# The layout of the first block's key and query loads, and the place of the iota, in a windowed attention kernel followed by a squared-ReLU MLP

## The chip, the cores and the metric

The kernel runs on one core of a Trainium2 chip. The metric is the device time of one execution in microseconds. The core has five engines that work through their own queues in order: PE (matmuls, with PEld for its weight loads), ACT (activations), DVE (vector work), POOL and SP. DMA transfers are issued from the queues of SP, ACT and POOL and are carried out by 16 DMA engines.

## The reference

Two layers in sequence. The first is causal attention with a window of 128 positions and a linear distance bias; the second is an MLP with a squared ReLU.

```python
batch, n_heads, seq, head_dim = (8, 8, 576, 64)
scores = scale * np.matmul(q, k.transpose(0, 1, 3, 2))
bias = slopes[:, None, None] * (-np.abs(rel))[None, :, :]
mask = (rel >= 0) & (rel < 128)
attn = softmax(np.where(mask, scores + bias, -1e9))
attn_out = np.matmul(attn, v)                        # 8 x 8 x 576 x 64
x = attn_out.transpose(0, 2, 1, 3).reshape(4608, 512)
out = np.maximum(x @ w_in, 0.0) ** 2 @ w_out         # 512 -> 2048 -> 512
```

All inputs and the output are float32 in DRAM; the kernel computes in bfloat16 with float32 accumulation.

## The kernel before, in words

**Blocks.** Each of the 8 batches has 576 positions, cut into blocks of 128 (the last one has 64). The kernel treats the first block of all batches first (blocks 0 to 7), then the others. For each block it loads k, q and v for all 8 heads. Blocks from 1 on are loaded by POOL's queue, which casts to bfloat16 on the way (L387 for k and q into `kq`, L392 for v into `vf` or `vt`). Block 0 is different: its k and q are loaded as float32 into `stage` by four transfers from the queues of SP and ACT (L373, one half r each), and DVE casts them into `kq` (L379). Its v comes from POOL like the others.

**From a block to x.** PE transposes `kq` (L443, group tp), ACT or DVE copies the result out of PSUM into `kqT` or `kqf` (L273, L271), PE computes the scores s (L499), ACT takes the exponential (L523), DVE multiplies with the masks (L531), PE multiplies with v (L566, group pv), DVE divides by the row sums (L584, L588), and PE transposes the result (L608, xp), which ACT or DVE copies into `xT`. From block 9 on, SP's transposing DMAs take the place of the PE transposes.

**The layout of block 0.** Its `kq` rows are not tokens. Each partition holds, for one head pair c and one group g of four neighbouring tokens, the 4 x 64 numbers of a head of the pair in each half r. So a row of `stage` is 1 KB of contiguous DRAM. `source` (L350) makes this view of DRAM, and the evacuation of the transposes (L451 to L458) puts the tokens back in order.

**The MLP.** Groups of 512 tokens go through w_in (L700 for the first three groups in narrower units, L716 afterwards), ACT's relu (L671), DVE's square (L662), w_out (L742), a copy to `osb` and a store by SP (L761). The weights are loaded in four quarters each by POOL, between the loads of the blocks, in the order of the list FIRST: b0, b1, b2, i0, i1, o0, i2, o1, b3, i3, o2, o3, b4 and so on, where b is a block, i a quarter of w_in and o one of w_out. Of b0, only v is on POOL's queue.

**What sets the order.** Every step is a task with a cost, a key and the tasks it depends on. A planner (L84) simulates the engines with these costs: at each turn it takes, among the tasks that could start within a small tolerance of the earliest, the one with the lowest key; where two engines could take a task at the same time and key, the first engine in its list gets it. The instructions are then emitted in the order of the planned starts, and each engine runs its own in that order. A DMA task is planned to follow the DMA tasks planned before it, one at a time (870 ns for a load of 128 rows from POOL, 330 ns for one of block 0's four loads). At most 8 DMAs are outstanding on POOL's side, and 8 on the side of SP and ACT. Where the planner sees a gap of more than 200 ns ahead of one of PE's early tasks, it puts filler matmuls on a zero tile there (L250 to L252), enough to fill 70% of the gap at full clock. Eight warm-up matmuls (L413) stand at the very start of PE's queue.

**The constants of the start.** `build_iota` (L286) writes the token distances on POOL. The identity for PE's transposes, the distance tile and through it the masks (L294, L300, L301, L310) are made from it by DVE and ACT. Its key is EARLY + IOTA (L290); v of block 0 has the key EARLY + 100.2, and the loads of block 1 EARLY + 200 and above.

Of the kernel before, what the change touches and what calls it, by code (L numbers as in the profile page):

```python
# [20 lines left out]
N_WARM = 8  # L21
FILL = 0.7
LEAD = 320
IOTA = 100.3
TP, XP = "h", "h"
UNITS = {0: 128, 1: 256, 2: 256}
CUT = 384
# [148 lines left out]
def kernel(  # L176
# [14 lines left out]
    C = d_model // 128  # L191
# [54 lines left out]
    def bank_of(slot, name):  # L246
        bank(slot, name)
        return slot

    def fill(task, slot):  # L250
        for _ in range(int(task.gap * FILL / 56.0) if task.gap > 200.0 else 0):
            nc.tensor.matmul(slot.tile[:, 0:128], warm[:, 0:128], warm[:, 0:128], start=True, stop=True)  # L252

    def tile_of(slot):
        return tiles[slot.tag][slot.idx]

    def act(n):
        return n * 0.95 + 115.0
# [4 lines left out]
    def dve_p(n, rate=1):  # L263
        return n / rate / 0.96 + 185.0

    def mm(n):
        return max(n, 66) / 2.4 + 2.5

    def copy(task, o, i):
        if task.eng == "DVE":  # L270
            nc.vector.tensor_copy(o, i)  # L271
        else:
            nc.scalar.activation(o, i, AF.Copy)  # L273
# [15 lines left out]

    t_iota = plan.add({"POOL": 400.0}, EARLY + IOTA, build_iota, name="iota")  # L290
    t_wz = plan.add({"DVE": 280.0}, EARLY, lambda: nc.vector.memset(warm, 0.0), name="warm0")
# [58 lines left out]
    def source(t, m, split=False):  # L350
        b, kb = seq[m]
        s = t[b, :, kb * 128:kb * 128 + blk[kb], :]
        if split:
            return s.rearrange("(c r) (g i) d -> c g r (i d)", r=2, i=4)
        return s.rearrange("h s d -> s h d")

    def load_block(m, key):
# [10 lines left out]
        if m == 0:  # L368
            t_l = []
            for i, src in enumerate((k, q)):  # L370
                for r, (eng, e) in enumerate((("SP", nc.sync), ("ACTQ", nc.scalar))):
                    def fetch(i=i, src=src, r=r, e=e):
                        e.dma_start(view(stage, i)[:, r], source(src, m, split)[:, :, r])  # L373
                    t_l.append(plan.add({eng: 450.0}, key + 0.1 * i, fetch, dma=330.0, lat=1000.0,
                                        name=f"l{'kq'[i]}{m}.{r}"))

            def cast_kq(i):
                w = slice(i * d_model, (i + 1) * d_model)
                nc.vector.tensor_copy(kq[s_kq[m].idx][:, w].rearrange("s (i r d) -> s r i d", i=4, d=D),  # L379
                                      stage[:, w].rearrange("s (r i d) -> s r i d", r=2, d=D))  # L380
            c_k = plan.add({"DVE": 480.0}, key, lambda: cast_kq(0), t_l[0:2], [s_kq[m]], name=f"ck{m}")
            c_q = plan.add({"DVE": 480.0}, key, lambda: cast_kq(1), t_l[2:4] + [c_k], name=f"cq{m}")
            t_kq[m] = [c_k, c_q]
        else:
            def fetch_kq():
                for i, src in enumerate((k, q)):
                    nc.gpsimd.dma_start(view(kq[s_kq[m].idx], i), source(src, m, split))  # L387
            t_kq[m] = [plan.add({"POOL": 1780.0}, key, fetch_kq, [], [s_kq[m]], dma=2 * ns,
                                name=f"lkq{m}", count=2)]

        def fetch_v():
            nc.gpsimd.dma_start(tile_of(s_v[m])[0:n, :, 0:D], source(v, m))  # L392
# [29 lines left out]
    def transpose_kq(m, due):  # L422
        n = blk[seq[m][1]]
        kb = seq[m][1]
        sT = s_kqT[m] = Slot("kqT" if kb else "kqT0")
        split = m == 0
        if m >= N_PE:
            def flip():
                nc.sync.dma_start_transpose(out=tile_of(sT)[:, :, 0:n], in_=kq[s_kq[m].idx][0:n, :])
            t_f = plan.add({"SP": 1500.0}, due - 60, flip, t_kq[m] + [t_zero if kb == HALF else None], [sT],  # L430
                           [s_kq[m]], dma=1700.0 * n / 128, name=f"kqT{m}")
            t_kqT[m] = [[t_f], [t_f]]
            return
        t_tp, evs = [None, None], [[], []]
        for i in range(2):
            st = Slot(TP if m else "o")

            def tp(i=i, st=st):
                fill(t_tp[i], bank_of(st, "tp"))
                st.tile = st.tile.bitcast(BF16)  # L440
                src = kq[s_kq[m].idx][:, i * d_model:(i + 1) * d_model]
                for j in range(C):
                    nc.tensor.transpose(st.tile[:, j * 128:(j + 1) * 128],  # L443
                                        src[:, j * 128:(j + 1) * 128], ident)
            t_tp[i] = plan.add({"PE": 4 * mm(128)}, due - 60 + i, tp,
                               [t_ident, t_tp[0] if i else last["tp"], t_kq[m][min(i, len(t_kq[m]) - 1)]],
                               [st] if i else [st, sT], [s_kq[m]] if i else [], name=f"tp{m}.{i}")

            pieces = [(0, C // 2), (C // 2, C)] if i and m == 0 else [(0, C)]
            for c0, c1 in pieces:  # L450
                def evac(i=i, st=st, c0=c0, c1=c1, e=len(evs[i])):  # L451
                    o = tile_of(sT)[:, i * C + c0:i * C + c1, 0:n]
                    if split:
                        src = st.tile[:, 0:512].rearrange("p (i c g) -> p c g i", i=4, c=C)[:, c0:c1]
                        o = o.rearrange("p c (g i) -> p c g i", i=4)
                    else:
                        src = st.tile[:, 0:512].rearrange("p (c s) -> p c s", c=C)[:, c0:c1, 0:n]
                    copy(evs[i][e], o, src)  # L458
                w = (c1 - c0) * n
                evs[i].append(plan.add({"ACT": act(w), "DVE": dve_p(w, 1 if split else 2)}, due - 58, evac,  # L460
                                       [t_tp[i]] + evs[i], [], [st], name=f"ev{m}.{i}"))
        last["tp"] = t_tp[1]
        t_kqT[m] = [[evs[0][0], evs[1][0]], evs[0] + evs[1]]
# [339 lines left out]
```

The softmax here doesn't subtract the row's maximum and nothing guards it: scores larger than these inputs give would overflow.

## Time and profile before

| what | value |
|---|---|
| three runs | 320.89, 321.00, 321.04 us (median 321.0) |
| the profiled execution | 320.97 us, span of its records 319.2 us |
| instructions | 7118 |
| DMA traffic | 39.14 MB in 164082 packets, mean 123 GB/s |
| k of block 0: issued by SP and ACT at | 0.74 us |
| q of block 0: issued by SP at, by ACT at | 1.53, 1.91 us |
| DVE's casts of k and q start at | 6.57, 10.63 us |
| first transposes of k and q on PE | 7.42, 11.11 us |
| first scores on PE | 12.61 us |
| first MLP matmuls (L700) | 19.07 us |
| POOL's start: v0, iota, k1, q1 | 1.25, 2.36, 2.66, 3.61 us |

The span counts from the first record of the profile to the last; the time of an execution is somewhat longer. The profile names groups by line, engine, operation and tiles. A name such as `PE h L700` stands for matmuls of line 700 that write the tile h. DMA share is the mean share of the 16 engines that is busy with packets; since several packets of one engine can be under way at once, it can go above 1. The chain of work is followed back from the last instruction: at each step to what released it or, without a wait, to the instruction before it on its engine.

### The profile page before, as it was taken

The page shows a single profiled execution, that of the slowest core. Times are in us where ns is not written, and L with a number is a line of the kernel's source. Part 1 is how long each engine was busy: PE and PEld are TensorE (multiplying, and loading weights), DVE is VectorE, ACT ScalarE, POOL GpSimd, SP SyncE. Part 2 cuts the span into 40 slices and gives each one's busy share as a digit, 9 for nine tenths or more (in the row PEclk, how much of TensorE's full clock was granted, in tenths as well). Part 3 has the DMA queues.
Part 4 walks back from the last instruction along what each step waited for, and adds up shares of the span by engine and source line. Part 5 has one row for each costly group of instructions (what it writes and reads, how often), then busy time and mean ns, then how long its engine had stood idle before and what let it go on. Part 6 is the DMA issues. An engine that isn't in the chain of part 4 may idle for free.

```text
span 319.2 us, 7118 instructions
## 1 busy us (share of the span) xinstructions
PE 304.4 (95%) x2778; PEld 177.4 (56%) x2820; DVE 172.7 (54%) x494; ACT 173.9 (54%) x340; POOL 105.4 (33%) x131
## 2 busy tenths in 40 slices
PE   5798999999999999999999999999999999999994
PEld 2597776767777755554555555554454444444442
DVE  2374566756766766767666666675664222222211
ACT  3376467658775547665665665655753444344300
POOL 8734498645440957203947006400000000000000
PEclk9999999999999999999999999999999999999999
DMA  8999999999999999949999929952121100010112
GB/s 96 174 204 190 179 156 184 152 169 141 206 165 145 159 171 205 163 69 148 169 195 167 135 69 157 184 132 61 42 65 36 49 34 33 35 33 34 66 68 66
DMA packets 164082, 39.14 MB, mean 123 GB/s; under 512 B 154704, under 2 KB 159568, under 8 KB 164048
## 3 DMA queue, kind: packets, MB, share of 16 engines
q0 software_dynamic: 114656, 18.10, 83.1%
q1 hardware_dynamic: 49128, 20.33, 32.5%
q8 instruction: 22, 0.36, 0.5%
q10 hardware_dynamic: 264, 0.26, 0.3%
q14 instruction: 12, 0.10, 0.1%
HBM read 36.70 MB, written 9.44 MB: 145 GB/s over the span
## 4 chain that ended last, share of the span: by engine, by line
PE 93%; DMA 3%; issue 1%; ACT 1%; DVE 1%; ACTq 0%
PE o L742 38%; PE h L716 26%; PE h L700 14%; PE pv L566 6%; PE s L499 6%; DMA stage<-in_q_dram 3%; PE tp L443 2%; PE xp L608 1%; PE pv L252 1%; ACT masks L310 0%; PE s L252 0%; ACTq L373 0%; ACT rt L671 0%; PE h L252 0%; DVE kq L379 0%
## 5 line engine op out<-in xcount | busy, mean ns | idle before, releaser
L742 PE MATMUL o<-w_out_sb,g 128*128 128x512 bf16 (+2 forms) x567 | 138.5, 373 | 2.4 <-issue 1.6
L671 ACT ACTIVATE rt<-h 128x512 bf16<-128x512 f32 x144 | 86.0, 610 | 93.0 <-PE h L716 65.4
L662 DVE TENSOR_TENSOR g<-rt 128x512 bf16<-128x512 bf16 x144 | 60.2, 421 | 75.7 <-ACT rt L671 75.6
L716 PE MATMUL h<-xT,w_in_sb 128*128 128x512 bf16 x367 | 95.5, 379 | 0.8
L742 PEld LDWEIGHTS <-g 128*128 128x128 bf16 x592 | 54.0, 98 | 55.6
L523 ACT ACTIVATE P<-s 128x512 bf16<-128x512 f32 (+1 forms) x136 | 67.1, 584 | 13.6 <-PE s L499 13.6
L716 PEld LDWEIGHTS <-w_in_sb 128*128 128x128 bf16 x384 | 35.2, 98 | 39.3
L531 DVE TENSOR_TENSOR P<-P,masks 128x512 bf16<-128x512 bf16 (+1 forms) x112 | 44.4, 405 | 14.3 <-ACT P L523 9.6
L700 PE MATMUL h<-xT,w_in_sb 128*128 128x128 bf16 (+1 forms) x512 | 46.7, 246 | 0.7 <-ACT rt L671 0.7
L392 POOL DMA_DIRECT2D vt<-in_v_dram x32 | 27.2, 851 | 57.6 <-PE pv L566 52.3
L387 POOL DMA_DIRECT2D kq<-in_k_dram x39 | 33.6, 861 | 24.7 <-DMA kqT<-kq 18.9
L700 PEld LDWEIGHTS <-w_in_sb 128*128 128x128 bf16 x512 | 38.7, 98 | 4.6 <-issue 0.8
L387 POOL DMA_DIRECT2D kq<-in_q_dram x39 | 33.7, 864 | 6.2 <-PE h L700 2.7
L588 DVE TENSOR_TENSOR x<-pv,rec 128x256 bf16<-128x256 f32 (+1 forms) x80 | 33.6, 422 | 2.6
L566 PEld LDWEIGHTS <-P 128*128 128x128 bf16 (+1 forms) x576 | 25.9, 101 | 14.8 <-DVE P L538 1.7
L584 DVE RECIPROCAL rec<-pv 128x4 f32<-128x4 f32 (+1 forms) x80 | 14.3, 179 | 20.8 <-PE pv L566 18.0
L566 PE MATMUL pv<-vt,P 128*128 128x65 bf16 (+1 forms) x448 | 24.6, 194 | 0.1
L273 ACT ACTIVATE osb<-o 128x512 f32<-128x512 f32 x23 | 14.0, 607 | 8.0 <-PE o L742 7.7
L499 PEld LDWEIGHTS <-kqT 64*128 64x128 bf16 x448 | 12.4, 94 | 7.3 <-issue 6.8
L271 DVE COPY osb<-o 128x512 f32<-128x512 f32 (+2 forms) x14 | 9.2, 654 | 12.8 <-PE o L742 12.6
L499 PE MATMUL s<-kqT 64*128 64x128 bf16 (+1 forms) x256 | 15.6, 210 | 0.0
L443 PE MATMUL tp<-ident,kq 128*128 128x128 bf16 x72 | 7.5, 239 | 4.8 <-DVE kq L379 4.8
(42 smaller groups left out, 110.2 us busy)
## 6 DMA issues: line engine op xcount, KB each, us to landing
out_dram<-osb SPq DMA_DIRECT2D x32, 256.0 KB, 3.6
kq<-in_k_dram POOLq DMA_DIRECT2D x31, 128.0 KB, 7.4
kq<-in_q_dram POOLq DMA_DIRECT2D x31, 128.0 KB, 7.4
vt<-in_v_dram POOLq DMA_DIRECT2D x24, 128.0 KB, 7.0
w_in_sb<-in_moe_w_in_dram POOLq DMA_DIRECT2D x4, 512.0 KB, 11.6
w_out_sb<-in_moe_w_out_dram POOLq DMA_DIRECT2D x4, 512.0 KB, 15.5
vf<-in_v_dram POOLq DMA_DIRECT2D x8, 128.0 KB, 9.0
out_dram<-osb SPq DMA_DIRECT2D x6, 128.0 KB, 2.3
```

Of the source, the lines that this page charges most:

```text
L387: nc.gpsimd.dma_start(view(kq[s_kq[m].idx], i), source(src, m, split))
L392: nc.gpsimd.dma_start(tile_of(s_v[m])[0:n, :, 0:D], source(v, m))
L499: nc.tensor.matmul(sS[2 * g2 + r].tile[:, jj * 256 + c0:jj * 256 + c0 + w], tile_of(s_kqT[mk])[rows, c, :], tile_of(s_kqT[mq])[rows, C + c ...
L523: nc.scalar.activation(flat(Pt[sP.idx]), sS[i].tile.rearrange("p (j t) -> p j t", j=2)[:, :, lo:hi], AF.Exp, bias=0.0, scale=scale)
L531: nc.vector.tensor_tensor(flat(Pt[sP.idx]), flat(Pt[sP.idx]), flat(masks), op=ALU.mult)
L566: nc.tensor.matmul(sv.tile[0:n, hi * (D + 1):(hi + 1) * (D + 1)], Pt[sP.idx][:, place(h)].rearrange("p t q -> p (t q)")[:, w], tile_of(s_v ...
L588: nc.vector.tensor_tensor(xt[sx.idx][0:n, hf * 256:(hf + 1) * 256].rearrange("p (h e) -> p h e", h=4), heads(sv)[0:n, :, 0:D], sr.tile[0:n ...
L662: nc.vector.tensor_tensor(o, i, i, op=ALU.mult)
L671: nc.scalar.activation(srt.tile, slot.tile, AF.Relu, bias=0.0, scale=1.0)
L700: nc.tensor.matmul(slot.tile[:, f * w:(f + 1) * w], w_in_sb[:, cc, fc * 128:(fc + 1) * 128], xT[:, cc, lo:lo + w], start=cc == 0, stop=cc ...
L716: nc.tensor.matmul(slot.tile, w_in_sb[:, cc, fc * 128:(fc + 1) * 128], xT[:, cc, g * 512:(g + 1) * 512], start=cc == 0, stop=cc == C - 1)
L742: nc.tensor.matmul(slot.tile[:, 0:hi - lo], gt[:, fc, t * 128:(t + 1) * 128], w_out_sb[:, fc, lo:hi], start=fc == 0, stop=fc == FCB - 1)
```

## The change

Two things are changed. In the view of DRAM that block 0's k and q are loaded through, the partition dimension is made of the token group g (32 of them) outermost and the head pair c (4) inside it, where before c was outermost. Row p of `stage` was c * 32 + g and is g * 4 + c. The evacuation of the transposes reads PSUM's columns in the new order, so that `kqf` holds the same as before. The four transfers, their issuing queues, their row size of 1 KB and the casts stay.

Second, the key of the iota is EARLY + 3 instead of EARLY + 100.3. It stood behind the load of block 0's v on POOL's queue and ahead of block 1's loads; now it stands ahead of both.

```diff
-IOTA = 100.3
+IOTA = 3
...
         if split:
-            return s.rearrange("(c r) (g i) d -> c g r (i d)", r=2, i=4)
+            return s.rearrange("(c r) (g i) d -> g c r (i d)", r=2, i=4)
...
                     if split:
-                        src = st.tile[:, 0:512].rearrange("p (i c g) -> p c g i", i=4, c=C)[:, c0:c1]
+                        src = st.tile[:, 0:512].rearrange("p (i g c) -> p c g i", i=4, c=C)[:, c0:c1]
                         o = o.rearrange("p c (g i) -> p c g i", i=4)
```

## The prediction

> **What bounds the kernel now.** I read the page from the engine shares down to the chain that ended last, then that chain in order of time over the first 30 us.
>
> ```profile
> PE 304.4 (95%) x2778; PEld 177.4 (56%) x2820; DVE 172.7 (54%) x494; ACT 173.9 (54%) x340; POOL 105.4 (33%) x131
> ...
> PE 93%; DMA 3%; issue 1%; ACT 1%; DVE 1%; ACTq 0%
> ```
>
> PE sets the end. The one other engine with a share is DMA, 3%, and the lines give it to one transfer, the first block's queries. Busy time by stretch (columns: PE, PEld, DVE, ACT, POOL, clock, DMA share, GB/s) shows where PE is loose:
>
> ```profile
> 0.00:26.98 26.98, 20.16 (x227) 14.84 (x229) 12.27 (x57) 14.02 (x42) 16.26 (x24) 1.00 1.34 160
> 26.98:319.20 292.22, 284.27 (x2551) 162.60 (x2591) 160.47 (x438) 159.88 (x299) 89.15 (x108) 1.00 1.15 119
> ```
>
> From 26.98 us on PE is 97% busy, so nothing but PE work can be saved there. Before that it stands 6.8 us, and of its 20.2 busy us 6.5 are filler matmuls (the group of L252, 64 of them) and 3.6 the warm-up: some 17 us are no work. Only a shift of this prologue can come out at the end. Its chain (start, length, what):
>
> ```profile
> 1.91 8.69 DMA stage<-in_q_dram
> 10.61 0.02 issue
> 10.63 0.44 DVE kq L379
> 11.07 0.05 issue
> 11.11 0.61 PE tp L443 x4
> 11.72 0.96 PE s L252 x9
> 12.68 0.33 PE s L499 x4
> ...
> 26.45 0.49 ACT rt L671
> 26.94 0.04 issue
> 26.98 3.02 PE h L700 x51
> ```
>
> The q load holds everything until 10.6. The second limit is hidden in POOL's waits. At most 8 of its DMAs are outstanding, so the wait of the ninth shows when the first has landed:
>
> ```profile
> 11.06 0.74 POOL L340 DMA_DIRECT2D w_in_sb<-in_moe_w_in_dram  x1 [2.32 <-DMA vf<-in_v_dram]
> ...
> 18.29 0.76 POOL L340 DMA_DIRECT2D w_in_sb<-in_moe_w_in_dram  x1 [1.61 <-DMA w_in_sb<-in_moe_w_in_dram]
> ...
> 20.83 0.74 POOL L343 DMA_DIRECT2D w_out_sb<-in_moe_w_out_dram  x1 [1.79 <-DMA w_in_sb<-in_moe_w_in_dram]
> ...
> 26.18 0.88 POOL L387 DMA_DIRECT2D kq<-in_k_dram  x1 [2.05 <-DMA w_in_sb<-in_moe_w_in_dram]
> ```
>
> Counting in issue order (v0, k1, q1, v1, k2, q2, v2, in0, in1, out0, in2, ...): v0 landed near 11.0, in0 near 18.25, in1 near 20.8, in2 near 26.15. The first L700 matmuls, which read in0, start at 19.07; the next 16, on in1, at 21.20; those on in2 at 26.98. So the prologue has two ropes: the q load, and the weight stream only 0.4 to 0.8 us behind it.
>
> **What the Trainium skill says.** "DMA: Bandwidth & Descriptors", section "Why a DMA increments its semaphore by 16 and not by 1": a DMA runs on the largest k up to 16 engines that divides the slowest dimension of both sides. The old view has 4 outermost, the destination 128 partitions: k=4. The trace agrees: between 2.5 and 3.5 us, with only ACT's k half running, the mean DMA share is 0.18, under 3 of 16 engines. The same page, "Issuing engines are not separate DMA queues": all queues interleave on the same engines, so the four also carry POOL's loads. The trace agrees: with q landed at 10.6, packets under 512 B (only block loads have those) still run at 317 in 12 to 13 us and 238 in 14 to 15, and end near 15.4, while weight rows begin near 11: a few engines lag by about 4 us. "SBUF — State Buffer", section "Who interferes with whom": a DVE cast in a two-port mode and GpSimd block each other. Agreeing: the k cast beside POOL's issues took 0.80 us, the q cast with POOL waiting 0.43. "TensorE: Matmul & The Clock Gate", Part 1: half clock until about 3.4 us of activity. Agreeing: fillers take 314 ns early and 218 ns from 16 us on.
>
> **The change part by part.**
>
> *Loads.* Each of the four stage loads keeps 128 rows of 1 KB, now with 32 outermost, so k=16: 8 rows per engine instead of 32. On the old four engines the four loads are 4 x 33 = 132 packets (data and semaphore); the 97 of ACT's queue between 2 and 4 us took 16.6% of 16 engines x 2 us, 55 ns each. So 7.2 us on each of the four, now 1.8 us on all sixteen. Can the issuing queue feed sixteen? The store at 312.7 us pushes 144 packets, 256 KB in 2 KB rows, through in under 1 us: yes. With the first packet at 2.4 us as now, k needs about 0.9 us of data and the slow ramp of today's first packets: landed at 3.3 to 4.6, taken 3.9 (today 6.55). q follows at 4.3 to 5.5, taken 4.7 (today 10.6).
>
> *Chain of block 0.* k cast 3.9 to 4.7 (0.80). The warm-up holds PE until 4.8; tp 4.8 to 5.4. q cast 4.7 to 5.5, at 0.80 since POOL now issues beside it: 0.37 us given back. tp of q 5.55 to 6.15. Fillers come from the planner's gaps: ahead of tp 1 they vanish, since it now books v0's transfer (870 ns) behind q's and so has q's cast done before tp 0 ends; about 9 stay ahead of s, 1.17 us at half clock: s at about 7.3, today 12.61. This rope moves 5.3 us; with q at 5.5, 4.5.
>
> *The evacuation's view.* Still one 512- or two 256-element PSUM reads (0.60 ACT, 0.76 DVE for the pair), only with c and g exchanged; innermost i steps 128 both ways: 0. If the layout cost anything, 0.2 us either way.
>
> *Iota first.* Iota (0.38 us) moves past one DMA issue on POOL's queue, v0's (1.03 us): iota to about 1.3, v0 to about 1.65; k1 stays at 2.66, since the sum ahead of it is the same. v0 lands at about 6 and is read at about 9.6: hidden. ident, dist and the table load come about a microsecond earlier, so ACT's masks end at 5.45 instead of 6.54, out of the way of the evacuation at 5.4. Without this, up to 1.1 us would come back; it is in the 5.3 already. SP's and ACT's queues keep their order; no wait is added.
>
> *Weight stream.* The four lagging engines lose 99 packets of 49 to 55 ns, 4.9 to 5.4 us each. The other twelve get 33, some 1.7 us, half of it ahead of 3.7 us, when POOL's packets start and they are idle. Without laggards the block loads end where the twelve end now, about 11; then in0 takes 2.5 us (the spacing of the weights' landings): 13.7 instead of 18.25. I take 4.5, with 4.0 (all of the twelve's extra felt) to 4.9 as bounds. Lanes free earlier too (v0 at 6, not 11), so POOL doesn't starve the stream.
>
> *Sum.* The ropes move 5.3 and 4.5. The first L700 goes to about 13.9, in1's to 16.6, and the dense stretch, now 0.83 behind in2 (ACT's 8 masks and a relu in front), starts between 26.98 - 5.3 (straight at in2) and 26.98 - 4.5. I take 4.7, nearer the stream. From there on PE is full and the loads behind move with the stream, so it stays: 319.2 - 4.7 = 314.5 of span. The profiled execution itself took 320.97, the runs 320.89 to 321.04 with median 321.0, so 1.8 us are added: **316.3 us**.
>
> **The rivals.**
>
> *The stream doesn't move (320.2).* If POOL's issues or HBM, and not the four engines, hold in0 at 18.25, q's early arrival is worth only the slack to it: 0.8 at the first unit. For it: POOL issues at 0.88 us per load without a gap until 8.7. Against it: the small packets trailing to 15.4. *Half of it (318.6):* the sixteen engines are so full that spreading only levels; 2.4 us remain.
>
> *No effect (321.0).* The transfer stays on four engines, say because the two sides' dimensions combine otherwise; iota alone buys nothing, since ACT's masks (to 6.54) are ready long before q.
>
> *Slower (323.2).* The planner re-times the start, and PE runs its queue strictly in order. If it now pulled block 4's transposes (L443, at 40.9) to the place of block 3's (30.5, or 25.8 after a shift of 4.7), PE would stand there for q4: issued at 29.72, 7.4 to land, 37.1, less 4.5, 32.6. That is 6.8 us of standing less 4.7 gained: 2.1 slower. It decides from a wait above 4.7 us. For it: the planner's load times are optimistic. Against it: from k1 on its times for POOL and for the DMA are the same sums in another order, so only block 0's steps are re-timed, by 0.75 us.
>
> **How the numbers follow.** Forecast (315.0 to 317.5, gains of 6.0 to 3.5: both ropes' bounds, and fewer half-clock matmuls since PE is busy from early on) 0.72; half 0.08; stream unmoved 0.08; no effect 0.04; slower 0.06; a gain above 6.0 0.02. The range 315.0 to 318.7 takes in forecast and half, 0.80. Within 0.2% (0.64 us, about what a measurement of this kernel can tell from no change) lies no effect: 0.04. The unmoved stream, 0.8, still counts as faster: 0.90. Slower 0.06.
>
> **What would show it.** Right: DMA share above 0.5 between 2.5 and 3.5 us; the k cast before 4.7 and the q cast by 5.6; s (L499) at 7 to 8; packets under 512 B gone by 12; POOL's wait for in0 ending near 13.7; PE dense from about 22.3; iota before v0 with k1 still at 2.66. Wrong: in0 still landing at 18, DMA share still 0.18, or a new PE wait above 1 us between 15 and 45 us.

## The result, and the profile after

| | before | after |
|---|---|---|
| runs | 320.81 to 321.04 us, median 320.94 (4) | 317.21 to 318.62 us, median 317.61 (4) |
| profiled execution, its span | 320.97, 319.2 us | 317.40, 315.6 us |

The ratio is 0.9901 with a 95% interval of 0.9877 to 0.9926: faster by 3.3 us, about 1%. In these runs the changed kernel scatters by 1.4 us and the old one by 0.2; larger sets of the old one scatter as much (31 runs: 320.68 to 323.17).

The chain that ended last, by engine, on the page of the changed kernel:

```profile
PE 86%; DMA 9%; POOL 2%; issue 0%; DVE 0%; POOLq 0%
```

DMA has 9% where it had 3%, although the kernel is faster. The chain in order of time (start, length, what) tells which transfers these are:

```profile
7.63 0.68 POOL w_in_sb L340
8.31 9.45 DMA w_in_sb<-in_moe_w_in_dram
17.75 0.28 issue
18.04 14.42 DMA w_out_sb<-in_moe_w_out_dram
32.46 0.04 issue
32.50 1.02 PE o L742 x4
...
36.61 5.98 DMA kq<-in_q_dram
42.58 0.05 issue
42.63 0.40 PE tp L443 x4
```

The load of q is gone from it. In its place the chain runs through POOL's queue: issue after issue, the landing of w_in's second quarter at 17.75 (in the short names of the prediction in1), which frees the lane for out2, out2's landing at 32.46, and a later block's q at 42.58. A lane is one of the at most 8 outstanding DMAs. POOL's own issues (start, length, what it is; the bracket says how long POOL stood and for what):

```profile
0.84 0.34 POOL L287 IOTA dist<- 128x256 f32 x1 [0.39 <-POOLq L787]
1.34 1.03 POOL L392 DMA_DIRECT2D vf<-in_v_dram  x1 [0.16 <-issue]
2.36 0.89 POOL L387 DMA_DIRECT2D kq<-in_k_dram  x1
...
14.51 0.76 POOL L340 DMA_DIRECT2D w_in_sb<-in_moe_w_in_dram  x1 [0.54 <-DMA w_in_sb<-in_moe_w_in_dram]
18.04 0.74 POOL L343 DMA_DIRECT2D w_out_sb<-in_moe_w_out_dram  x1 [2.77 <-DMA w_in_sb<-in_moe_w_in_dram]
20.02 0.74 POOL L343 DMA_DIRECT2D w_out_sb<-in_moe_w_out_dram  x1 [1.24 <-DMA w_out_sb<-in_moe_w_out_dram]
22.82 0.88 POOL L387 DMA_DIRECT2D kq<-in_k_dram  x1 [2.05 <-DMA w_in_sb<-in_moe_w_in_dram]
```

The same four waits stood at 18.29, 20.83, 23.39 and 26.18 before. So the weights land 2.8 to 3.8 us sooner, and k1 is issued at 2.36, not 2.66. PE in the stretches where it meets them, after:

```profile
14.34 1.05 PE L700 MATMUL h<-xT,w_in_sb 128*128 128x128 bf16 x16
...
22.54 3.75 PE L700 MATMUL h<-xT,w_in_sb 128*128 128x128 bf16 x64 [0.70 <-ACT rt L671]
...
30.01 1.96 PE L700 MATMUL h<-xT,w_in_sb 128*128 128x128 bf16 x32 [0.33 <-DMA w_in_sb<-in_moe_w_in_dram]
...
32.50 1.02 PE L742 MATMUL o<-w_out_sb,g 128*128 128x512 bf16 x4 [0.29 <-DMA w_out_sb<-in_moe_w_out_dram]
```

The same work before:

```profile
19.07 1.05 PE L700 MATMUL h<-xT,w_in_sb 128*128 128x128 bf16 x16
...
26.98 3.75 PE L700 MATMUL h<-xT,w_in_sb 128*128 128x128 bf16 x64 [0.70 <-ACT rt L671]
...
34.06 1.96 PE L700 MATMUL h<-xT,w_in_sb 128*128 128x128 bf16 x32
...
36.27 1.02 PE L742 MATMUL o<-w_out_sb,g 128*128 128x512 bf16 x3
```

There PE waits for no weights. (A few matmuls can be missing from a trace, hence x3 and x4.) The shift of the PE work can be read off: 4.73 us at the first L700, 4.44 at the dense stretch (the 64 matmuls in a row), 4.05 at the units on in3 (the 32 matmuls), 3.77 at out2's first use (L742), and 3.55 from the first 128x256 matmuls of L700 on (54.08 to 50.53) until the end. The gain is made in the prologue, and 0.9 us of it is lost again between 22 and 42 us.

That the loads are spread shows in the DMA view of 2.5 to 3.5 us (queue, packets, MB, share of 16 engines; q10 is ACT's queue, q1 SP's):

```profile
q10 hardware_dynamic: 176, 0.16, 57.5%
q1 hardware_dynamic: 144, 0.13, 38.2%
```

Before, the same microsecond had only this:

```profile
q10 hardware_dynamic: 42, 0.04, 17.7%
```

The packet counts say the same: ACT's queue, which carries two of the four loads, has 264 packets on the page before and 288 after. With 128 rows to a load that is 132 and 144 for each, so 4 and 16 beyond the rows, as the prediction's sum of data and semaphore packets has it for 4 and 16 engines. k is cast at 3.75 instead of 6.57, q at 6.25 instead of 10.63.

### The profile page after: what moved, and what is told of

It reads as the page before. It is cut to its first block, busy times and chain, and to the rows that moved or that the text cites. A ratio compares the mean times of both kernels' runs of the same rounds, so it can differ in the third digit from the quotient of the medians.

```text
span 315.6 us, 7140 instructions
## 1 busy us (share of the span) xinstructions
PE 306.2 (97%) x2810; PEld 176.3 (56%) x2810; DVE 173.4 (55%) x494; ACT 173.5 (55%) x340; POOL 105.4 (33%) x131
## 4 chain that ended last, share of the span: by engine, by line
PE 86%; DMA 9%; POOL 2%; issue 0%; DVE 0%; POOLq 0%
PE o L742 38%; PE h L716 27%; PE h L700 10%; PE pv L566 6%; PE s L499 5%; DMA w_out_sb<-in_moe_w_out_dram 5%; DMA w_in_sb<-in_moe_w_in_dram 3%; DMA kq<-in_q_dram 2%; POOL kq L387 1%; POOL vf L392 1%; PE tp L443 0%; PE xp L608 0%; POOL w_in_sb L340 0%; POOL dist L287 0%; DVE osb L271 0%
## 5 line engine op out<-in xcount | busy, mean ns | idle before, releaser
L742 PE MATMUL o<-w_out_sb,g 128*128 128x512 bf16 (+2 forms) x592 | 143.0, 373 | 0.3 <-DMA w_out_sb<-in_moe_w_out_dram 0.3
L716 PE MATMUL h<-xT,w_in_sb 128*128 128x512 bf16 x384 | 96.7, 379 | 0.0
L742 PEld LDWEIGHTS <-g 128*128 128x128 bf16 x592 | 54.0, 98 | 55.9 <-issue 0.4
L700 PE MATMUL h<-xT,w_in_sb 128*128 128x128 bf16 (+1 forms) x512 | 46.8, 246 | 1.1 <-ACT rt L671 0.7
L700 PEld LDWEIGHTS <-w_in_sb 128*128 128x128 bf16 x512 | 38.6, 98 | 5.2 <-DMA w_in_sb<-in_moe_w_in_dram 1.4
L273 ACT ACTIVATE osb<-o 128x512 f32<-128x512 f32 x23 | 13.9, 606 | 8.0 <-PE o L742 7.7
L499 PE MATMUL s<-kqT,kqT 64*128 64x128 bf16 (+1 forms) x192 | 11.4, 209 | 0.0
```

The lines of the kernel that those rows point to most:

```text
L499: nc.tensor.matmul(sS[2 * g2 + r].tile[:, jj * 256 + c0:jj * 256 + c0 + w], tile_of(s_kqT[mk])[rows, c, :], tile_of(s_kqT[mq])[rows, C + c ...
L700: nc.tensor.matmul(slot.tile[:, f * w:(f + 1) * w], w_in_sb[:, cc, fc * 128:(fc + 1) * 128], xT[:, cc, lo:lo + w], start=cc == 0, stop=cc ...
L716: nc.tensor.matmul(slot.tile, w_in_sb[:, cc, fc * 128:(fc + 1) * 128], xT[:, cc, g * 512:(g + 1) * 512], start=cc == 0, stop=cc == C - 1)
L742: nc.tensor.matmul(slot.tile[:, 0:hi - lo], gt[:, fc, t * 128:(t + 1) * 128], w_out_sb[:, fc, lo:hi], start=fc == 0, stop=fc == FCB - 1)
```

## The experiments

Two theories are tested. *Stream:* the end is set by when weights and blocks land on POOL's queue; the change takes packets off four engines that lagged, and block 0's own steps have slack. *Chain:* q's arrival and the steps behind it set the end. Gains below are against the runs of the kernel before in the same batch (medians 321.05 to 321.41).

| run | median us | ratio, 95% interval | gain us |
|---|---|---|---|
| changed kernel again | 317.54 | 0.9894, 0.9882 to 0.9907 | 3.5 |
| layout alone | 318.68 | 0.9921, 0.9905 to 0.9937 | 2.5 |
| iota alone | 321.08 | 0.9996, 0.9987 to 1.0005 | 0.1 |
| iota second, new order | 318.72 | 0.9928, 0.9912 to 0.9944 | 2.3 |
| two iotas | 318.22 | 0.9911, 0.9890 to 0.9931 | 3.2 |
| extra loads on 4 engines | 321.69 | 1.0010, 1.0000 to 1.0020 | -0.5 |
| the same on 16 | 318.70 | 0.9916, 0.9897 to 0.9936 | 2.6 |
| only k spread | 319.06 | 0.9940, 0.9928 to 0.9953 | 2.0 |
| only q spread | 318.82 | 0.9927, 0.9915 to 0.9939 | 2.2 |
| q's cast later | 317.72 | 0.9897, 0.9877 to 0.9917 | 3.5 |
| half of out1 left out | 316.58 | 0.9852, 0.9838 to 0.9865 | 4.8 |
| second masks later | 319.64 | 0.9946, 0.9933 to 0.9958 | 1.8 |

**The control.** The changed kernel, unaltered.

> The changed kernel once more, as the control for the runs beside it: both theories 317.2 to 318.2 us.

It came to 317.54 us, four runs within 317.49 to 318.33.

**Each part alone.** First the layout:

```diff
-IOTA = 3
+IOTA = 100.3
```

> The new layout with the iota's old key, so also with the planner's old order. Two theories. Stream: the end is set by when the weights and blocks land on POOL's queue, and the change speeds this up by taking packets off four laggard engines; the start of block 0 has slack. Chain: the end is set by q's arrival and the steps of block 0 behind it. Stream: about 317.6 us as the changed kernel, 317.2 to 318.2. Chain: the masks and the fillers ahead of q's transposes (9 of about 130 ns) come back, so about 1 us slower than the changed kernel, 318.6.

Measured 318.68: the number that the chain named (318.6), but not for its reason. PE's timeline of this kernel:

```profile
12.78 0.29 PE L566 MATMUL pv<-vf,P 128*128 128x65 bf16 x4
15.68 1.26 PE L700 MATMUL h<-xT,w_in_sb 128*128 128x128 bf16 x16 [2.61 <-DMA w_in_sb<-in_moe_w_in_dram]
```

All that stands ahead of the first L700 is done at 13.1, 1.4 us sooner than with both parts (14.5), and PE then stands 2.61 us for in0. The chain is early and the stream late. My stream number was wrong because I took POOL's landings as unmoved by the iota: POOL's wait for in0 ends at 15.91 here, at 14.51 with both parts. Then the iota alone:

```diff
-IOTA = 100.3
+IOTA = 3
 ... (loads of k and q as in the kernel before)
```

> The iota's new key with the old layout, so the planner's new order but the loads on four engines. Stream and chain both: no gain, 320.5 to 321.3, since q lands at 10.6 and the laggards stay. If the planner's new order is what gains, it is near 317.6.

Measured 321.08, no gain. With the loads on four engines, neither the planner's new order nor the earlier constants buy anything. In its trace the dense stretch even starts at 26.45, half a microsecond sooner than before, and PE then stands for in3:

```profile
34.24 1.96 PE L700 MATMUL h<-xT,w_in_sb 128*128 128x128 bf16 x32 [0.64 <-DMA w_in_sb<-in_moe_w_in_dram]
```

**Which part of the iota's move.** The key changes both POOL's queue and the planner's order, so the emission alone was swapped:

```diff
+        at_v0 = next(t for t in done if t.name == "lv0")
         for t in done:
-            t.emit()
+            if t is t_iota:
+                at_v0.emit()
+            if t is not at_v0:
+                t.emit()
```

> The changed kernel with the planner's new order on every engine, but the iota put behind v0's load on POOL's queue again. Stream: POOL's loads from k1 on start 0.3 us later and the weights land later by that or more: 317.9 to 318.7 us. If the planner's order of the start was what the iota's key bought: as the changed kernel, 317.6.

318.72, as slow as the layout alone, so the planner's order is not what the key bought. The swap makes both POOL's loads and the masks late (ACT's masks end at 6.54, after the full change at 5.13), but PE stands for a weight:

```profile
15.75 1.75 PE L700 MATMUL h<-xT,w_in_sb 128*128 128x128 bf16 x16 [2.47 <-DMA w_in_sb<-in_moe_w_in_dram]
```

A second iota behind v0 delays POOL alike but leaves the masks early:

```diff
             t.emit()
+            if t.name == "lv0":
+                nc.gpsimd.iota(spare, pattern=[[-128, 2], [1, 128]], base=128, channel_multiplier=-1,
+                               allow_small_or_imprecise_dtypes=True)
```

> The changed kernel with a second iota, into a tile that nobody reads, behind v0's load on POOL's queue: the masks and the planner's order stay as changed, only POOL's loads from k1 on start 0.3 us later. Stream, by POOL's timing: 317.9 to 318.7 us, as with the iota put second. If the late masks were what cost there: 317.5.

The median 318.22 lies inside the stream's span, but single runs go from 317.63 to 319.73, and the interval overlaps the control's as well as that of the iota put second: POOL's 0.3 us is not shown to be the cause. What does differ in the traces is the rate at which data arrive. For 11 to 12 and 12 to 13 us, first the changed kernel, then the layout alone:

```profile
DMA packets 224, 0.20 MB, mean 202 GB/s; under 512 B 30, under 2 KB 224, under 8 KB 224
DMA packets 205, 0.21 MB, mean 207 GB/s; under 512 B 3, under 2 KB 205, under 8 KB 205
```

```profile
DMA packets 272, 0.15 MB, mean 149 GB/s; under 512 B 144, under 2 KB 272, under 8 KB 272
DMA packets 186, 0.19 MB, mean 190 GB/s; under 512 B 0, under 2 KB 186, under 8 KB 186
```

With the iota second (swapped emission) the loads moved 133, 146, 180, 164 and 193 GB/s in the five microseconds from 10 on, where the changed kernel had 179, 202, 207, 205 and 207: 184 KB less, which is 0.9 us at 205 GB/s. The profiled execution with two iotas, one of its fastest, had no such dip, although k1 was issued at 2.68 there, as late as in the two that had it. POOL's wait for in2 ended at 23.25 in it, as in the other traces with the iota ahead of v0 and the stage loads spread (22.82 to 23.28), but at 23.79 and 24.10 in the two with v0 ahead. As far as these few traces go, the dip goes with v0 ahead of the iota rather than with k1's 0.3 us; why is open.

**The laggards.** Three more loads of 128 rows of 1 KB into a tile that nobody reads, issued by SP behind q's, first in the old view (4 engines), then in the new one (16). The lines that call it behind q's first load are left out:

```diff
+            def again():
+                for i, r in ((0, 0), (0, 1), (1, 0)):
+                    s = (k, q)[i][0, :, 0:128, :].rearrange("(c r) (g i) d -> c g r (i d)", r=2, i=4)
+                    nc.sync.dma_start(view(spare, i)[:, r], s[:, :, r])
...
```

> The changed kernel with three more loads of 128 rows of 1 KB in the old view (four engines), read by nobody, on SP's queue behind q's: about 99 more packets on each of four engines, as many as the change took away. Stream: the gain is gone, 320.3 to 321.2, with in2 landing near 26 again although q's cast is still at about 6.3 to 7. Chain: q is ahead of them, so 317.6 to 318.3.

> The same three unread loads as in the run with four engines loaded again, same bytes, same queue, same issue times, but in the new view, so on 16 engines. If it is the four laggards that made that run lose 4.1 us: here only the bytes are felt, 384 KB at some 300 GB/s, 1.2 us, so 318.2 to 319.2 us. If the bytes themselves did it: 321.2 to 322.

321.69 on four engines, half a microsecond above the stream's span, and 318.70 on sixteen: the same bytes, the same queue, 3 us apart (2.6 of gain against -0.5). So of the 4.0 us that the extra loads cost on four engines, some 0.9 is bytes and 3.1 is their concentration. On four engines, DVE, POOL and PE show how the start stood (line numbers differ in this kernel by 7):

```profile
6.03 0.43 DVE L386 CAST kq<-stage 128x512 bf16<-128x512 f32 x1 [1.64 <-DMA stage<-in_q_dram]
```

```profile
26.97 0.89 POOL L394 DMA_DIRECT2D kq<-in_k_dram  x1 [2.06 <-DMA w_in_sb<-in_moe_w_in_dram]
12.93 0.40 PE L450 MATMUL tp<-ident,kq 128*128 128x128 bf16 x4 [3.13 <-DMA kq<-in_q_dram]
```

q's cast is at 6.03, earlier than in the changed kernel, and POOL's wait for in2 ends at 26.97, later than before the change (26.18). The stream is not only weights: PE stands 3.13 us for block 1's q, which also comes over POOL's queue. An early q with a late stream gains nothing.

**Half the spreading.** k in the new view and q in the old, and the reverse (the choice by tensor and the evacuation's view are left out here):

```diff
-            return s.rearrange("(c r) (g i) d -> g c r (i d)", r=2, i=4)
+            return s.rearrange("(c r) (g i) d -> " + ("g c" if g_out else "c g") + " r (i d)", r=2, i=4)
...
```

> Only k's loads in the new view (16 engines), q's in the old one (4 engines); planner's order as changed. The four engines keep half of their extra packets. Stream: about half of the gain, 319.0 to 319.8 us. Chain: q lands late (8 to 9), so 1.5 to 2.5 us of the 3.5 are gone, 319.1 to 320.1.

> Only q's loads in the new view, k's in the old one; the same packets on the four engines as with only k. Stream: the same as with only k, 319.0 to 319.8 us. Chain: q lands soon after k (6.5 to 7.5), so close to the changed kernel, 317.6 to 318.6.

319.06 and 318.82, with overlapping intervals, though q's cast starts at 8.82 in the first and at about 7.8 in the second, behind k's. The chain asked of the second to be near the changed kernel; it is 1.3 us from it. The stream asked for 319.0 to 319.8: the first is inside, the second 0.2 below. Both lie a little below the middle between 317.5 and 321: half the packets off the four engines give some 60% of the gain.

**q later, transfers untouched.**

```diff
+                if i:
+                    nc.vector.tensor_copy(spare, stage[:, w])
+                    nc.vector.tensor_copy(spare, stage[:, w])
                 nc.vector.tensor_copy(kq[s_kq[m].idx][:, w]. ...
```

> The changed kernel with two copies of q's staged rows (128x512 float32, some 0.5 us each) on DVE ahead of q's cast: q's chain is about 1 us later, no transfer is touched. Stream: 317.6 to 318.1, since the stretch behind the weights' landings has up to 0.9 us of slack that the loads take anyway. Chain: 318.6 or more, one for one.

DVE's timeline:

```profile
6.32 0.70 DVE L381 COPY spare<-stage 128x512 f32<-128x512 f32 x1 [1.93 <-DMA stage<-in_q_dram]
7.05 0.84 DVE L382 COPY spare<-stage 128x512 f32<-128x512 f32 x1
7.81 0.41 DVE L383 CAST kq<-stage 128x512 bf16<-128x512 f32 x1
```

The cast is 1.6 us later and the median 317.72, the control's gain to 0.1 us. Three of four runs lie at 317.55 to 317.78. The fourth, which is the profiled one, took 318.6, the chain's number: there the first L700 starts at 16.41 without a wait for in0 and the dense stretch at 24.33, so in this execution the chain did cost, although what ended last there still runs over out2's landing (at 33.87). How much slack q has is not settled; the ropes lie within a microsecond or two of each other.

**Where the 0.9 us went.** Two of the four row blocks of out1 are not loaded and are zero, so their part of the product is left out:

```diff
...
-                nc.gpsimd.dma_start(w_out_sb[:, 4 * n:4 * n + 4, :],
-                                    moe_w_out[n * w:(n + 1) * w, :].rearrange("(c p) f -> p c f", p=128))
+                m = 2 if n == 1 else 4
+                nc.gpsimd.dma_start(w_out_sb[:, 4 * n:4 * n + m, :],
+                                    moe_w_out[n * w:n * w + 128 * m, :].rearrange("(c p) f -> p c f", p=128))
```

> The changed kernel with half of the second quarter of w_out (rows 768 to 1023, 512 KB in DRAM) left out of its load and zero instead, so the part of the product that these rows make is left out. Everything behind it on POOL's queue lands some 1.3 us sooner. Stream: PE's waits at in3, out2 and a q of a later block (0.3 + 0.3 + 0.2 us, 0.9 of shift lost between 22 and 42 us) go: 316.6 to 317.0 us. If the 0.9 us are lost to something else: 317.5.

316.58 us, at the edge of the stream's span, and 1.3 us more gain than the control's where 0.9 had been lost. PE's waits of this kernel, longest first, have no load behind in0 any more (line numbers differ by 1; the columns are total, times and longest; the last, shorter line is left out):

```profile
PE tp L444 <- DVE kq L380: 2.1, 1, 2.1
PE wm L414 <- DVE warm L291: 1.2, 1, 1.2
PE h L701 <- DMA w_in_sb<-in_moe_w_in_dram: 0.7, 1, 0.7
PE h L701 <- ACT rt L672: 0.7, 1, 0.7
...
```

The dense stretch starts at 23.10, the units on in3 at 30.17 and the 128x256 matmuls at 50.02: the lead over before is 3.88 us at the first and 4.06 at the last, where the changed kernel went from 4.44 to 3.55. So the loss between 22 and 42 us is waiting for the stream, and a shorter stream brings it back.

**Masks out of the way.** ACT's eight second masks stand ahead of the relu that PE waits 0.70 us for at 22.54:

```diff
-                                later=0.0 if part else 18000.0)
+                                later=0.0 if part else 36000.0)
```

> The changed kernel with the second half of the masks (8 exponentials of 0.21 us on ACT, now at 20.3 us and in front of the relu that PE waits 0.7 us for) planned later. Stream: the dense stretch may start up to 0.5 us sooner, but in3 lands when it lands: 317.3 to 317.7 us. Chain: 316.8 to 317.0.

319.64, 1.7 us less gain than the control's; both theories missed it. The dense stretch starts at 22.50, no sooner, since in2 holds it. The masks run at 38.9 to 40.6 instead, in front of two relus, and the 128x256 matmuls start at 52.02 (50.53): the planner's order around them changed too, and the two were not told apart.

## Why the prediction was right or wrong

The forecast was 316.3 us, 4.7 gained; 3.3 to 3.5 were measured, inside the range. The mechanism was right: the four engines were relieved, and with them the weights came sooner. One term was too large, and one loss was not looked for.

*Loads.* Sixteen engines and k's landing (3.7 for 3.9) were right. Small packets are not only those of block loads, as I had said: of the 38 under 512 B between 2.5 and 3.5 us after, POOL's queue had at most 4. The trail to 15.4 before stands all the same: 317 of them in 12 to 13 us, 3 after. q landed at 6.2, not 4.7: 213 of the four loads' 576 packets were still to come at 3.5 us, when POOL's begin, and shared the engines with these. It did not matter at the first L700, which starts at 14.34 when in0 has only just landed (issued at 7.57, 6.7 us to landing).

*Chain.* s came at 7.93 for 7.3 although q's cast was 1.5 us late, because of a second error that offset the first: the nine fillers ahead of s took 0.67 us, not 1.17. One filler followed the other every 56 ns there and every 107 ns before (estimated from nine in a row less the length of the last). It is this spacing that shows the half clock; the 314 and 218 ns of a single filler are not in the ratio of two. The first L700 at 14.34 for 13.9 was set as much by in0 as by the chain.

*Weight stream.* This is the term that was mis-sized: 4.5, bounds 4.0 to 4.9. POOL's waits for in0 to in2 ended 2.8 to 3.8 us sooner. From the four engines' 4.9 to 5.4 us I had to take what the other twelve now carry, 1.7, and credited half of that to idle time before 3.7 us. My lower bound of 4.0 was said to take off all of it, but 4.9 to 5.4 less 1.7 is 3.2 to 3.7, which is what came. The runs with extra loads show that bytes are felt even when spread: 0.9 us for 384 KB, so by estimate 1.2 for the 512 KB of the four loads.

*Slack.* The work at the first L700 and the dense stretch moved 4.73 and 4.44 us, close to the 4.7 that I took, but partly by luck. POOL issues some time behind a landing, so the landings that I read from its waits were 0.25 to 0.5 us late. By the DMA view in0, in1 and in2 landed at 18.0, 20.6 and 25.6 before (issue plus time to landing: 7.93 + 10.1, 11.06 + 9.5, 12.52 + 13.1), and at 14.3, 17.75 and 22.3 after. So the dense stretch stood 1.4 us behind in2, not 0.83, and stands 0.3 behind it now: in2 gave 3.4 of its 4.44 us, and used-up slack the rest. My reading of in1 was also wrong: the matmuls at 21.20 were the second block's on in0. in1's first use stood at 22.26, 1.7 us behind its landing; in the changed kernel it is at 17.80, on a landing at 17.75.

*"It stays".* Wrong: 0.9 of the 4.44 us at the dense stretch is lost to waits for in3 (0.33), out2 (0.29) and a later q. I had seen PE full behind 27 us and did not ask whether the loads there moved as far as the work did.

*Iota.* I gave its move up to 1.1 us, and without it 1.0 to 1.2 us of the gain are missing: the size is right by luck, since the way was not. I had the masks standing in front of the evacuation; with the layout alone and with the iota second, PE stands 2.61 and 2.47 us for in0, so there the weights are late and not the masks. "k1 stays at 2.66" was wrong too: the iota runs in time in which POOL stood anyway (idle until 1.25 before), and k1 is issued at 2.36. How the order of v0 and the iota makes the weights about 1 us later was not settled.

*Rivals.* A stream that does not move and no effect are refuted by the landings. "Half" (2.4 us) is at the edge of the interval, 2.4 to 3.9 us, and its reason is in part true: bytes are felt on all sixteen engines too. The planner's order for PE did not pull any waiting load forward: from the first L700 on, PE's order of work is the same in both kernels.

## What to carry to other kernels

In this kernel, transfers that ran on 4 of the 16 DMA engines were paid twice: they were slow themselves (q's cast at 10.63 us, with sixteen engines at 6.25), and later transfers landed when their share on those four engines landed (small packets until 15.4 us, afterwards until 12). Read the outermost dimension of both sides of a load, 4 here before and 32 after, and look in the DMA view for small packets that trail long after the others. When such laggards are freed, do not expect their own time back (4.9 to 5.4 us here) but that less what the other engines take over (3.2 to 3.7); then ask whether the loads behind move as far as the work that will now meet them earlier.

## What the runs showed that was not expected

The number of a run can fit a theory whose mechanism the same run refutes: the layout alone took what the chain had named (318.7), with PE standing 2.61 us for a weight. And the place of one instruction of 0.34 us was worth a microsecond: with the iota behind v0, the loads moved 133 to 193 GB/s in the five microseconds from 10 on, where the full change had 179 to 207, and 1.0 to 1.2 us of the gain are gone. The cause of this is open, and so is that of the changed kernel's scatter (317.21 to 318.62): its two traced executions took 317.40 and 317.50, so none of its longer ones can be looked into.
